# Side loads of a decode-attention backward pass, moved from SyncE's load queue to GpSimd's store queue

## The chip, the cores and the metric

The kernel runs on one core of a Trainium2 chip. A core has five engines with instruction streams of their own: TensorE (PE; its weight loads are shown as PEld), VectorE (DVE), ScalarE (ACT), GpSimd (POOL) and SyncE (SP). They wait for each other through semaphores. 16 DMA engines move data between the chip's main memory and the on-chip buffers. A transfer is issued by an instruction of SP, ACT or POOL and then lies in that engine's DMA queue; an engine issues its transfers in the order of its own instruction stream, and an instruction that waits holds up all that stand behind it. The metric is the device time of one execution in microseconds (us), the median of several runs.

## The reference

The forward pass is a conditioned block: `mod = silu(c) @ w_mod` gives six vectors; then layer norm, attention of one query row against a key and value cache (32 heads, 8192 positions, 192 numbers a head), and a small MLP. What is computed is the output and the gradients of nine of the inputs:

```python
h = _layernorm(x, axis=-1) * (1 + ca) + sa
x = x + ga * _A_ref(h, A_k_cache, A_v_cache, A_wq, A_wo)   # softmax(q k) v @ wo, q = h @ wq
h = _layernorm(x, axis=-1) * (1 + cb) + sb
x = x + gb * _B_ref(h, B_w1, B_w2, B_w3, B_w4)
...
_out, _vjp = jax.vjp(_f, A_x, A_k_cache, A_v_cache, A_wq, A_wo, B_w3, B_w4, c, w_mod)
_grads = _vjp(grad_out)
```

The two caches are 100.7 MB each, and so are their gradients dK and dV. One query row makes all products rank one, so the kernel moves much and computes little for each byte.

## The kernel before, in words

**Stage one** (to about 560 us) runs the forward pass over the heads: K and V tiles come in through SP, and nothing large goes out.

**Stage two** (the rest) runs backward over 64 half heads. The loop `for s in range(NS)` counts them in s; one s handles a tile of 128 x 32 x 192 numbers, 1.57 MB. For each s it reads one V tile, five ahead (`load_v`, L328, on SP), multiplies it by a row of the gradient on DVE (`mul_q`, L1092), sums on PE (`tree_q`, L1111), makes dP and dS on DVE (L347, L1458), writes a dK tile on DVE (`dk_part`, L1127) and a dV tile on PE and ACT (`dv_groups`, L1122 and L1123), and stores both through POOL (`dk_store`, L1412, and `dv_store`, L1408). The stores leave from five buffers used in turn (KC, VB2, QT, KE, KD; the trace names them by their tiles KB, VB and qs_bc), so a dK or dV write can wait until an earlier store from the same buffer has landed.

**Side work** is cut into steps by hand and laid into the loop. `at(s0, n, g)` puts n steps of a generator g at the times s0, s0 + 0.25, ... in units of s; `slot()` is called four times in each s and takes the steps that are due. So a plan time of 8.5 means the third slot of s = 8, which stands behind `dk_store(8)` and ahead of `dv_store(8)` in the text. One s takes some 12.5 us. The side work is:

- `g_ld(n)` loads a tile of wo (0.49 MB, `load_wo`, L203, SP), `g_do(n)` transposes it on PE (L903) for the next pair of heads, and `g_dwo(n)` overwrites it with the gradient of wo (DVE, L1255) and stores it (L1225, POOL). There are two buffers, wo_st, so a load waits until the store of the tile before the last has landed.
- `g_dq` and `g_wm` work on chunks of wq and w_mod (0.98 MB each, 13 in all). `next_w()` (L1152, SP) loads the chunk after the present one into one of two buffers, w_st and stg; the first transposes that read it come a little over two s later. The chunk is overwritten with its gradient and stored by `put` (L1225).
- Four finished stores (two tiles of dwo, two chunks of dw_mod) are held back in a list and issued near the end by `g_held` (L1229, POOL).

The order of the instructions is fixed as written for four engines, and not for POOL:

```python
ORDER = {mybir.EngineType.PE, mybir.EngineType.DVE, mybir.EngineType.Activation, mybir.EngineType.SP}
...
ctx.enter_context(tc.manual_schedule(engines=ORDER))
```

POOL's own order is chosen when the kernel is built.

Of the kernel before, what the change touches and what calls it, by code (L numbers as in the profile page):

```python
# [20 lines left out]
def kernel(  # L21
# [26 lines left out]
    nc = tc.nc  # L48
# [16 lines left out]
    NT = HQ // 2  # L65
    PW = 2 * DH
    CW = 2 * PW
# [49 lines left out]
    def tcol(n, name, dtype=FP32):  # L117
        return tmp.tile([P, n], dtype, name=name)
# [34 lines left out]
    def layernorm_bwd(dn, n, r, add, out, name):  # L153
        pr = col(2 * ND, "lb_pr")
        V_.tensor_copy(out=pr[:, 0:ND], in_=dn)
        V_.tensor_tensor(out=pr[:, ND : 2 * ND], in0=dn, in1=n, op=ALU.mult)
        s = mean_cols(pr, 2, "lb_s")
        t1 = col(ND, "lb_t1")
        V_.tensor_scalar(out=t1, in0=n, scalar1=s[:, 1:2], scalar2=s[:, 0:1], op0=ALU.mult, op1=ALU.add)
        t2 = col(ND, "lb_t2")  # L160
        V_.tensor_tensor(out=t2, in0=dn, in1=t1, op=ALU.subtract)
        V_.scalar_tensor_tensor(out=out, in0=t2, scalar=r[:, 0:1], in1=add, op0=ALU.mult, op1=ALU.add)
# [13 lines left out]
    def store_vec(src, dram, name):  # L176
        tp = psS.tile([NF, P], FP32, name="sv_t", tag="s")
        T_.transpose(out=tp[0:ND, :], in_=src, identity=ident_f)
        rows = tmp.tile([ND, P], BF16, name="sv_rows", tag="rows")
        V_.tensor_copy(out=rows, in_=tp[0:ND, :])  # L180
        nc.gpsimd.dma_start(out=dram.rearrange("o (i p) -> (o i) p", p=P), in_=rows)
# [4 lines left out]
    wo_v = A_wo.rearrange("(t p c) r -> t p c r", p=P, c=3)  # L186
# [8 lines left out]
    def load_w(view3, lo, hi):  # L195
        w = wst.tile([P, ND, CW], BF16, name="w_st", tag="w", bufs=1)
        nc.sync.dma_start(out=w[:, :, 0 : hi - lo], in_=view3[:, :, lo:hi])
        return w

    def load_wo(t):  # L200

        w = wst.tile([P, 3, D], BF16, name="wo_st", tag="wo")
        nc.sync.dma_start(out=w, in_=wo_v[t])  # L203
        return w


# [120 lines left out]
    def load_v(h, t, v):  # L327
        nc.sync.dma_start(out=v, in_=V_hd[h][:, t * JH : (t + 1) * JH, :])  # L328
        return v
# [25 lines left out]
    TL = NT - 1  # L355
# [20 lines left out]
    with tc.tile_pool(name="vs", bufs=3) as vsp, tc.tile_pool(name="ft", bufs=2) as ft, \  # L376
            tc.tile_pool(name="psM", bufs=2, space=PS) as psM, tc.tile_pool(name="psO", bufs=2, space=PS) as psO, \
            tc.tile_pool(name="psR", bufs=2, space=PS) as psR:
        def load_k(h, t):
            kb = KB[(2 * h + t) % NKB]  # L380
            if (h, t) == (H1, 1):
                for j in (0, JQ):
                    nc.sync.dma_start(out=kb[:, j : j + JQ, :], in_=K_hd[h][:, JH + j : JH + j + JQ, :])
            else:
                nc.sync.dma_start(out=kb, in_=K_hd[h][:, t * JH : (t + 1) * JH, :])
            return kb
# [131 lines left out]
        w = load_w(wq_v, 0, CW)  # L518
# [3 lines left out]
        X, os_, wo_l = {0: {"k": [load_k(0, 0), load_k(0, 1)], "v": [load_v(0, 0, VB[0])]}}, {}, {}  # L522
# [15 lines left out]
        with tc.manual_schedule(engines=ORDER):  # L538
            for i in range(H1):
# [4 lines left out]
                t = (i - 4) // 2  # L544
                late = i % 2 == 0 and t >= 0
# [402 lines left out]
            def dw4_dve(dst, a0, lo, hi):  # L948
                for a in range(lo, hi):
                    V_.tensor_scalar(out=dst[:, (a - a0) * D : (a - a0 + 1) * D], in0=dbo_bc, scalar1=g_[:, a : a + 1], scalar2=None, op0=ALU.mult)  # L950

            def dw4_store(dst, lo, n):
                nc.gpsimd.dma_start(out=dw4_v[:, lo : lo + n, :], in_=dst[:, 0 : n * D].rearrange("p (a r) -> p a r", a=n))
# [87 lines left out]
    def do_of(h):  # L1041
        return do_r[:, (TL - h // 2) % NDR, (h % 2) * DH : (h % 2 + 1) * DH]
# [101 lines left out]
    def next_w():  # L1144
        if wseq:
            view, n = wseq.pop(0)
            if cur.setdefault("n", 0) % 2 == 0:
                w = wst.tile([P, ND, CW], BF16, name="w_st", tag="w", bufs=1)
            else:
                w = bst.tile([P, ND, CW], BF16, name="stg")  # L1150
            cur["n"] += 1
            nc.sync.dma_start(out=w, in_=view[:, :, n * CW : (n + 1) * CW])  # L1152
            cur["next"] = w

    def g_bcast(src, n, out):
# [21 lines left out]
        yield  # L1177

    def g_ld(n):
        wo_l[TL - n] = load_wo(TL - n)  # L1180
        yield

    def g_chunk(b, first, v3, rows, dst, n, acc, lay):
# [43 lines left out]
    def g_held():  # L1227
        out, w = held.pop(0)
        nc.gpsimd.dma_start(out=out, in_=w)  # L1229
        yield  # L1230

    def g_dq(t):
        acc = tcol(3, "dq_acc")
        if t == TL:
            V_.tensor_copy(out=acc, in_=dq_x)
        for lo, hi, M, b in ((0, P, M1[:, 2 * t, 0:DH], 0), (0, P, M1[:, 2 * t + 1, 0:DH], 2), (0, 64, M2[0:64, t, 0:DH], 1), (64, P, M2[64:128, t, 0:DH], 1)):
            h = 2 * t + (1 if (b == 2 or lo == 64) else 0)
            if h == H1:
                continue
            junk = bst.tile([P, DH], FP32, name="dq_junk")  # L1240
            V_.tensor_tensor_reduce(out=junk[lo:hi, :], in0=M, in1=do_of(h)[lo:hi, :], scale=1.0, scalar=0.0, op0=ALU.mult, op1=ALU.add, accum_out=acc[lo:hi, b : b + 1])
        dq = tcol(3, "dq")
        V_.scalar_tensor_tensor(out=dq, in0=acc, scalar=SCALE, in1=ckS[:, 3 * t : 3 * t + 3], op0=ALU.mult, op1=ALU.subtract)
        yield from g_chunk(t % 2, t % 2 == 1, dq, ha, dwq_v, t // 2, dha, HEADS)

    def g_wm(n):
        for b in range(2):
            g = 2 * n + b
            yield from g_chunk(b, b == 0, dmod[:, 3 * g : 3 * g + 3], sc, dwm_v, n, dsc, PLAIN)
# [29 lines left out]
    def g_dw3(lo, n):  # L1279
        dw3_v = out_6.rearrange("(i p) n -> p i n", p=P)  # L1280
        o3 = bst.tile([P, ND, CW], BF16, name="stg").rearrange("p a r -> p (a r)")
        for i in range(n):
            V_.tensor_scalar(out=o3[:, i * F : (i + 1) * F], in0=du_bc, scalar1=n2[:, lo + i : lo + i + 1], scalar2=None, op0=ALU.mult)
        if lo == 0:
            dw4_dve(o3[:, n * F : n * F + D], 11, 11, 12)
            dw4_store(o3[:, n * F : n * F + D], 11, 1)
        nc.gpsimd.dma_start(out=dw3_v[:, lo : lo + n, :], in_=o3[:, 0 : n * F].rearrange("p (a r) -> p a r", a=n))
        if lo + n == ND:
            next_w()
        yield  # L1290

    def g_finish_x():
        V_.tensor_copy(out=d_sa, in_=dha)
        V_.tensor_tensor(out=d_ca, in0=dha, in1=n0, op=ALU.mult)
        d_n0 = tcol(ND, "d_n0")
        V_.scalar_tensor_tensor(out=d_n0, in0=ca, scalar=1.0, in1=dha, op0=ALU.add, op1=ALU.mult)
        dx = tcol(ND, "dx")
        layernorm_bwd(d_n0, n0, r0, dx1, dx, "lb0")
        yield
        store_vec(dx, out_1[0], "dx")  # L1300
        yield

    def g_finish_c():
        t = tcol(ND, "dc_t")
        V_.tensor_scalar(out=t, in0=sig, scalar1=-1.0, scalar2=1.0, op0=ALU.mult, op1=ALU.add)
        V_.tensor_tensor(out=t, in0=t, in1=c_c, op=ALU.mult)
        V_.scalar_tensor_tensor(out=t, in0=t, scalar=1.0, in1=sig, op0=ALU.add, op1=ALU.mult)
        V_.tensor_tensor(out=t, in0=t, in1=dsc, op=ALU.mult)
        store_vec(t, out_8, "dc")
        yield  # L1310
# [4 lines left out]
    def at(s0, n, g):  # L1315
        plan.extend((s0 + 0.25 * k, g) for k in range(n))

    CW0, CWS, DO0 = 14.0, 3.5, 16.5
    d = g_do(1)
# [5 lines left out]
    d = g_do(2)  # L1325
# [2 lines left out]
    at(6.5, 1, g_dwo(1))  # L1328
    at(6.75, 4, g_bcast(du, NF, du_bc))
    at(7.75, 1, g_dw3(0, 2))  # L1330
    at(8.0, 1, g_ld(3))
    at(8.25, 2, g_small())
    at(8.75, 1, g_dwo(2))
    at(9.0, 3, g_do(3))
    at(9.75, 1, g_dw3(2, 2))
    at(10.0, 1, g_dwo(3))
    at(10.75, 1, g_ld(4))
    at(11.25, 1, g_dw3(4, 1))
    at(13.0, 3, g_do(4))
    at(13.75, 1, g_dwo(4))  # L1340
    for n in range(5, NT):
        d = DO0 + CWS * (n - 5) if n < NT - 2 else 47.75 + 0.75 * (n - NT + 2)
        at(d - 3.25, 1, g_ld(n))
        at(d, 3, g_do(n))
        at(d + 0.75, 1, g_dwo(n))
    late = list(range(GX, NWM))
    k, t = 0, TL
    while t >= 0 or late:
        if t >= 0 and not (late and k % 3 == 2):
            wseq.append((wq_v, t // 2))  # L1350
            at(CW0 + CWS * k, 5, g_dq(t))
            at(CW0 + CWS * k + 1.25, 5, g_dq(t - 1))
            t -= 2
        else:
            wseq.append((wm_v, late[0]))
            at(CW0 + CWS * k, 10, g_wm(late.pop(0)))
        k += 1
    at(CW0 + CWS * k - 1.0, 2, g_finish_x())
    for n in range(GX):
        wseq.append((wm_v, n))  # L1360
        at(CW0 + CWS * k, 10, g_wm(n))
        k += 1
    at(CW0 + CWS * k - 1.0, 1, g_finish_c())
    for s0 in (60.25, 60.75, 61.25, 62.25):
        at(s0, 1, g_held())
    plan.sort(key=lambda p: p[0])
    NP = len(plan)
# [83 lines left out]
    for s in range(NS):  # L1451
        h, t = ht(s)
# [6 lines left out]
            out=dS4,  # L1459
# [111 lines left out]
```

## Time and profile before

| what | value |
|---|---|
| median of 3 runs | 1391.4 us (1387.59 to 1393.44) |
| the profiled execution | 1390.66 us |
| its span, first to last instruction | 1388.9 us |
| DMA moved | 569.38 MB, mean 410 GB/s |
| q1, SP's queue | 342.03 MB, 60.0% of the DMA engines' span |
| q0, POOL's queue | 224.89 MB, 38.6% |
| busy share PE / DVE / ACT / POOL | 84% / 80% / 66% / 8% |
| granted TensorE clock, mean | 0.732 |

The profile is of one execution. Times in it count from the first instruction; 1.8 us of the execution lie outside the span. The view of stretches gives, for each stretch of time, each engine's busy time (with the number of instructions in brackets), the granted TensorE clock, the busy share of the 16 DMA engines and the rate in GB/s. The view of waits gives, for an engine and a line, what it waited for, the total, the number of waits and the longest. The timeline gives start, duration, engine, line and operation; a DMA's row is its issue, not its transfer. "POOLq" and "SPq" are the queues' own instructions.

### The profile page before, as it was taken

To read this page: it belongs to the slowest core of one execution; us is meant where nothing else is said; L and a number is where in the kernel's file an instruction comes from. 1 tells how busy PE (TensorE), PEld (TensorE's weight loads), DVE (VectorE), ACT (ScalarE), POOL (GpSimd) and SP (SyncE) were. 2 spreads that over 40 slices of the span, in tenths; PEclk is the share of its full clock that TensorE was granted. 3 is DMA by queue.
4 is the path that set the end of the run, shared out by engine and by line. 5 is a ranking of instruction groups with operands and counts; after the bars stand their busy time and mean duration, and the time that the engine had idled before them with its cause. 6 is when DMAs were issued, how large, how long until landed. Compare 5 with 4: busy or idle time off the path is not lost.

```text
span 1388.9 us, 30507 instructions
## 1 busy us (share of the span) xinstructions
PE 1163.4 (84%) x12712; PEld 735.9 (53%) x12712; DVE 1109.2 (80%) x1455; ACT 911.8 (66%) x2007; POOL 108.1 (8%) x196
## 2 busy tenths in 40 slices
PE   3989989999998999988868888788579896987974
PEld 2777777778787777633323444344334343433421
DVE  4999989999999999976757676677577766876784
ACT  0777777777777778866545666566466565755754
POOL 0000000000000000111111111011011111110011
PEclk8999999999999999755555565555665555755555
DMA  9999999999999999699999999999999999999989
GB/s 381 398 422 425 418 408 411 423 421 415 424 418 422 414 417 380 231 421 426 424 424 425 427 423 427 425 422 415 425 408 424 412 421 392 417 426 423 425 359 379
DMA packets 76872, 569.38 MB, mean 410 GB/s; under 512 B 7422, under 2 KB 25198, under 8 KB 37182
## 3 DMA queue, kind: packets, MB, share of 16 engines
q1 hardware_dynamic: 51594, 342.03, 60.0%
q0 software_dynamic: 24624, 224.89, 38.6%
q8 instruction: 99, 1.62, 0.4%
q10 hardware_dynamic: 516, 0.51, 0.1%
q14 instruction: 39, 0.32, 0.1%
HBM read 340.97 MB, written 226.44 MB: 409 GB/s over the span
## 4 chain that ended last, share of the span: by engine, by line
issue 41%; DVE 25%; DMA 18%; PE 8%; POOL 5%; ACT 1%; POOLq 0%; SPq 0%; DVEq 0%; ACTq 0%
DVE prod L333 10%; DMA KB<-in_A_k_cache_dram 9%; DVE prod L337 5%; DMA out_dram<-KB 5%; DMA out_dram<-qs_bc 4%; DVE vs L403 4%; PE mp L425 2%; POOL out_dram L1412 2%; PE half_ps L343 2%; POOL out_dram L1408 2%; PE mp L430 1%; POOL out_dram L1225 1%; DVE KB L1127 1%; DVE pq L1092 1%; DMA w4b<-in_B_w_dram 1%
## 5 line engine op out<-in xcount | busy, mean ns | idle before, releaser
L1111 PE MATMUL dot_ps<-pq,ident_bf 128*128 128x256 bf16 x1494 | 369.9, 389 | 27.4 <-DVE dP L347 25.6
L410 ACT ACTIVATE vs<-VB,Ef 128x192 bf16<-128x192 bf16 x840 | 303.6, 447 | 0.0
L1123 ACT CAST KB<-dv_ps 128x768 bf16<-128x768 f32 x312 | 241.1, 806 | 82.7 <-PE dv_ps L1122 81.9
L1111 PEld LDWEIGHTS <-ident_bf 128*128 128x128 bf16 x1494 | 148.2, 122 | 176.1 <-issue 139.2
L1122 PE MATMUL dv_ps<-do_r,er_b 1*128 1x192 bf16 x2016 | 223.5, 331 | 4.3 <-ACT KB L1123 2.7
L333 DVE TENSOR_TENSOR prod<-KB,qs_bc 128x6144 bf16<-128x6144 bf16 x62 | 207.9, 3352 | 24.1 <-DMA KB<-in_A_k_cache_dram 20.4
L1127 DVE TENSOR_TENSOR KB<-qh,dS 128x3072 bf16<-128x3072 bf16 x74 | 128.1, 1753 | 97.7 <-DMA out_dram<-KB 79.9
L425 PE MATMUL mp<-vs,KB 128*128 128x193 bf16 x1984 | 188.8, 247 | 3.9 <-ACT vs L410 2.6
L425 PEld LDWEIGHTS <-KB 128*128 128x128 bf16 x1984 | 168.6, 97 | 13.0 <-DMA KB<-in_A_k_cache_dram 5.3
L904 ACT COPY wT<-wT_ps 128x1024 bf16<-128x1024 bf16 x82 | 79.1, 964 | 108.4 <-PE wT_ps L903 108.1
L1122 PEld LDWEIGHTS <-er_b 1*128 1x128 bf16 x2016 | 69.1, 104 | 142.4 <-issue 139.9
L343 PE MATMUL half_ps<-prod,ident_bf 128*128 128x256 bf16 x744 | 95.1, 279 | 43.3 <-DVE prod L337 43.2
L403 DVE TENSOR_TENSOR vs<-VB,E 128x1728 bf16<-128x1728 bf16 x120 | 123.7, 1052 | 0.3 <-ACT vs L410 0.3
L1092 DVE TENSOR_TENSOR pq<-VB,do_r 128x3072 bf16<-128x3072 bf16 x66 | 115.5, 1750 | 0.0
L337 DVE TENSOR_TENSOR prod<-prod 128x3072 bf16<-128x3072 bf16 x62 | 108.7, 1754 | 1.0
L1092 DVE TENSOR_TENSOR pq<-KB,do_r 128x3072 bf16<-128x3072 bf16 x62 | 108.4, 1749 | 0.0
L430 PE MATMUL mp<-vs,KB 128*64 128x193 bf16 x1968 | 105.7, 250 | 0.0
L343 PEld LDWEIGHTS <-ident_bf 128*128 128x128 bf16 x744 | 72.9, 100 | 61.7 <-issue 52.9
L1123 ACT CAST VB<-dv_ps 128x768 bf16<-128x768 f32 x96 | 75.1, 806 | 38.1 <-PE dv_ps L1122 37.8
L1123 ACT CAST qs_bc<-dv_ps 128x768 bf16<-128x768 f32 x104 | 80.3, 806 | 24.8 <-PE dv_ps L1122 24.3
L390 ACT ACTIVATE E<-S_h,negm 128x256 bf16<-128x256 f32 x31 | 15.8, 508 | 113.8 <-DVE negm L561 111.5
L430 PEld LDWEIGHTS <-KB 128*64 128x64 bf16 x1968 | 78.8, 109 | 19.8 <-issue 19.4
(380 smaller groups left out, 1212.3 us busy)
## 6 DMA issues: line engine op xcount, KB each, us to landing
VB<-in_A_v_cache_dram SPq DMA_DIRECT2D x93, 1536.0 KB
out_dram<-KB POOLq DMA_DIRECT2D x74, 1536.0 KB, 18.0
KB<-in_A_k_cache_dram SPq DMA_DIRECT2D x63, 1536.0 KB
KB<-in_A_v_cache_dram SPq DMA_DIRECT2D x29, 1536.0 KB
out_dram<-qs_bc POOLq DMA_DIRECT2D x25, 1536.0 KB, 16.9
out_dram<-VB POOLq DMA_DIRECT2D x25, 1536.0 KB, 18.1
wo_st<-in_A_wo_dram SPq DMA_DIRECT2D x31, 480.0 KB
w_st<-in_A_wq_dram SPq DMA_DIRECT2D x12, 960.0 KB
```

The costliest lines, as they stand in the source:

```text
L333: V_.tensor_tensor(out=prod, in0=src, in1=vec[:, None, :].to_broadcast([P, JH, DH]), op=ALU.mult)
L337: V_.tensor_tensor(out=prod[:, :, 0:HW], in0=prod[:, :, 0:HW], in1=prod[:, :, DH - HW : DH], op=ALU.add)
L343: T_.matmul(ps, lhsT=ident_bf, rhs=prod[:, :, k : k + TF], start=(k == 0), stop=(k == w - TF))
L403: V_.tensor_tensor(out=vs[:, 0:n, 0:DH].rearrange("p j (a b) -> p j a b", b=4), in0=v[:, v0 : v0 + n, :].rearrange("p j (a b) -> p j a b", ...
L410: A_.activation(out=vs[:, k, 0:DH], in_=v[:, v0 + k, :], func=ACT.Copy, scale=Ef[:, j0 + k : j0 + k + 1])
L425: T_.matmul(mp[:, 0:MW], lhsT=kb[:, j0 + k, 0:P], rhs=vs[:, k, 0:MW], start=(q == 0 and k == 0), stop=(z and k == JQ - 1), skip_group_chec ...
L430: T_.matmul(mp[p0 : p0 + 64, MO : MO + MW], lhsT=kb[:, j0 + k, P:DH], rhs=vs[:, k, 0:MW], start=False, stop=(z and k >= JQ - 2), skip_grou ...
L1092: V_.tensor_tensor(out=pq[:, q], in0=v_l[s][:, q * JQ : (q + 1) * JQ, :], in1=do_of(ht(s)[0])[:, None, :].to_broadcast([P, JQ, DH]), op=AL ...
L1111: T_.matmul(ps[:, q * JQ : (q + 1) * JQ, :], lhsT=ident_bf, rhs=pq[:, q, :, k : k + TS], start=(k == 0), stop=(k == w - TS), skip_group_ch ...
L1122: T_.matmul(ps[:, b, k * DH : (k + 1) * DH], lhsT=er[p0 : p0 + 1, 2 * m + k, :], rhs=doh[p0 : p0 + 1, :], start=True, stop=True)
L1123: A_.copy(out=dV4[:, 2 * q : 2 * q + 2, m * PW : (m + 1) * PW], in_=ps[:, :, 0:PW])
L1127: V_.tensor_tensor(out=dK[:, lo:hi, :].rearrange("p j (a b) -> p j a b", b=4), in0=qh.rearrange("p (a b) -> p a b", b=4)[:, None, :, :].to ...
```

## The change

wq and w_mod chunks (all 13) and the wo tiles from n = 3 on (13 of them) are loaded through POOL's queue, where only stores are now. The tiles n = 1 and 2 stay on SP, as do all V tiles. Some steps move in the plan:

- `g_ld(3)` from 8.0 to 8.5; `next_w` after the last dw3 store becomes a step of its own, a quarter of an s later;
- wo tile 13: its three steps from 44.5 to 44.0, tile 15 from 48.5 to 49.0, with its load 2.25 instead of 3.25 ahead of it (46.75 instead of 45.25);
- the chunks of the end from 49.0, 52.5 and 56.0 to 49.75, 53.0 and 56.25; `g_finish_x` from 51.5 to 52.25, `g_finish_c` from 58.5 to 58.75;
- the held stores from 60.25, 60.75, 61.25 and 62.25 to 58.0, 58.0, 58.75 and 60.25.

```diff
-    def load_wo(t):
+    def load_wo(t, eng=nc.sync):
         w = wst.tile([P, 3, D], BF16, name="wo_st", tag="wo")
-        nc.sync.dma_start(out=w, in_=wo_v[t])
+        eng.dma_start(out=w, in_=wo_v[t])
...
-            nc.sync.dma_start(out=w, in_=view[:, :, n * CW : (n + 1) * CW])
+            nc.gpsimd.dma_start(out=w, in_=view[:, :, n * CW : (n + 1) * CW])
...
-        wo_l[TL - n] = load_wo(TL - n)
+        wo_l[TL - n] = load_wo(TL - n, nc.gpsimd if n > 2 else nc.sync)
...
         nc.gpsimd.dma_start(out=dw3_v[:, lo : lo + n, :], in_=o3[:, 0 : n * F].rearrange("p (a r) -> p a r", a=n))
+        yield
         if lo + n == ND:
             next_w()
-        yield
+            yield
...
-    at(8.0, 1, g_ld(3))
+    at(8.5, 1, g_ld(3))
...
-    at(11.25, 1, g_dw3(4, 1))
+    at(11.25, 2, g_dw3(4, 1))
...
-        d = DO0 + CWS * (n - 5) if n < NT - 2 else 47.75 + 0.75 * (n - NT + 2)
-        at(d - 3.25, 1, g_ld(n))
+        d = DO0 + CWS * (n - 5) if n < NT - 3 else (44.0, 47.75, 49.0)[n - NT + 3]
+        at(d - (3.25 if n < NT - 1 else 2.25), 1, g_ld(n))
...
+    cw = [CW0 + CWS * i for i in range(10)] + [49.75, 53.0, 56.25]
...
-    at(CW0 + CWS * k - 1.0, 2, g_finish_x())
+    at(cw[k] - 0.75, 2, g_finish_x())
...
-    at(CW0 + CWS * k - 1.0, 1, g_finish_c())
-    for s0 in (60.25, 60.75, 61.25, 62.25):
+    at(58.75, 1, g_finish_c())
+    for s0 in (58.0, 58.0, 58.75, 60.25):
         at(s0, 1, g_held())
```

In the lines left out, `CW0 + CWS * k` becomes `cw[k]`.

More of the change, by code (lines that the diff above doesn't have):

```diff
@@ L1350 @@
             wseq.append((wq_v, t // 2))
-            at(CW0 + CWS * k, 5, g_dq(t))
-            at(CW0 + CWS * k + 1.25, 5, g_dq(t - 1))
+            at(cw[k], 5, g_dq(t))
+            at(cw[k] + 1.25, 5, g_dq(t - 1))
             t -= 2
@@ L1355 @@
             wseq.append((wm_v, late[0]))
-            at(CW0 + CWS * k, 10, g_wm(late.pop(0)))
+            at(cw[k], 10, g_wm(late.pop(0)))
         k += 1
-    at(CW0 + CWS * k - 1.0, 2, g_finish_x())
+    at(cw[k] - 0.75, 2, g_finish_x())
     for n in range(GX):
         wseq.append((wm_v, n))
-        at(CW0 + CWS * k, 10, g_wm(n))
+        at(cw[k], 10, g_wm(n))
         k += 1
-    at(CW0 + CWS * k - 1.0, 1, g_finish_c())
-    for s0 in (60.25, 60.75, 61.25, 62.25):
+    at(58.75, 1, g_finish_c())
+    for s0 in (58.0, 58.0, 58.75, 60.25):
         at(s0, 1, g_held())
```

## The prediction

> **What bounds the kernel now.** I read the page's slices first. Their DMA row shows the 16 DMA engines full nearly throughout; POOL and SP do little else than issue transfers, and PE, DVE and ACT all have idle time. So the time is the bytes at some 424 GB/s, plus whatever makes the DMA engines run dry. I then cut the last 260 us into stretches of 5 us and looked for low rates (columns: us, five engines with counts, clock, DMA share, GB/s):
>
> ```profile
> 1165.00:1170.00 5.00, 5.00 (x45) 2.35 (x44) 0.00 (x0) 2.72 (x4) 0.00 (x0) 0.50 1.01 422
> 1170.00:1175.00 5.00, 3.81 (x27) 1.33 (x25) 2.40 (x2) 3.76 (x5) 0.00 (x0) 0.50 0.87 354
> 1175.00:1180.00 5.00, 0.00 (x0) 0.00 (x0) 4.91 (x14) 0.14 (x1) 1.11 (x2) 0.50 0.94 276
> 1180.00:1185.00 5.00, 4.37 (x32) 2.28 (x32) 4.88 (x8) 2.13 (x3) 0.00 (x0) 0.57 0.93 352
> ...
> 1325.00:1330.00 5.00, 0.48 (x5) 0.21 (x5) 4.43 (x13) 0.00 (x0) 0.53 (x1) 0.50 0.61 256
> 1330.00:1335.00 5.00, 4.86 (x33) 2.01 (x30) 4.54 (x5) 3.57 (x5) 0.92 (x2) 0.50 0.78 321
> 1335.00:1340.00 5.00, 5.00 (x33) 1.53 (x30) 4.97 (x5) 3.49 (x5) 0.44 (x2) 0.50 0.76 322
> 1340.00:1345.00 5.00, 4.69 (x29) 2.04 (x30) 4.93 (x6) 3.64 (x6) 1.29 (x3) 0.50 0.86 358
> ```
>
> Two holes. Between 600 and 1170 every stretch has a DMA share of 0.98 or more: there nothing can be gained except by moving bytes faster. What opens the holes is in the waits of DVE and of SP's queue:
>
> ```profile
> DVE KB L1127 <- DMA out_dram<-KB: 79.9, 21, 10.6
> SPq L203 <- DMA out_dram<-wo_st: 38.7, 4, 22.7
> SPq L1152 <- DMA out_dram<-stg: 26.2, 5, 9.0
> ```
>
> Compute waits for stores to land, never for a V tile: no V load is a releaser in DVE's list. And SP, in order, once stands 22.7 us behind one wo load that waits for a store; the V load behind it comes late:
>
> ```profile
> 1150.67 0.33 SPq L328 DMA_DIRECT2D VB<-in_A_v_cache_dram  x1
> 1173.71 0.33 SPq L203 DMA_DIRECT2D wo_st<-in_A_wo_dram  x1
> 1174.13 1.14 SPq L328 DMA_DIRECT2D VB<-in_A_v_cache_dram  x1
> ```
>
> This is tile 15 (load at 45.25), which takes the buffer of tile 13, stored by the step at 45.25 as well (POOL issue 1157.16).
>
> **The change part by part.** The sum is made against the profiled execution, 1390.66 us, which is 0.7 below the median of 1391.4.
>
> *The hole at 1170.* Against 424 GB/s the three stretches lack 70, 148 and 72 GB/s: 290 x 5 / 424 = 3.4 us. SP no longer waits there, its V load (3.7 us of work) can start near 1165, when DVE has freed the buffer, and tile 15 is loaded 2.0 s after tile 13's store (46.75 against 44.75), some 25 us, where such stores land in 9.0 to 24.1 us. Between 0 and -3.4, I take **-3.4**.
>
> *The hole at 1325.* 168, 103, 102 and 66 GB/s are lacking: 439 x 5 / 424 = 5.2 us. DVE had waited until 1324.14 for a store, then no stores were ready. The held stores, 2 x 0.49 and 2 x 0.98 MB or 7.0 us of DMA, now come at 1341.65 to 1359.04, when DMA is full again (423 GB/s from 1345). At 58.0 the two wo stores stand right behind the dV store at 1315.08 and fill 2.3 us of the first stretch; the chunk at 58.75 stands behind 1334.59 and fills some 2 more; the fourth, at 60.25, replaces a wo store. The last ACT copy ends at 1372.3 and the DMA engines drain for 13 us more, so what they do earlier comes off the end. Between 0 and -5.2, I take **-4.3**.
>
> *The fourth wo tile (n = 3).* Before, SP issued it at 660.91 and PE waited only 0.4 us for it at 672.81. Now it stands in POOL's queue at 8.5, right behind this dK store:
>
> ```profile
> 669.39 0.56 POOL L1412 DMA_DIRECT2D out_dram<-qs_bc  x1 [9.02 <-DVE x L1274]
> 670.48 0.53 POOL L181 DMA_DIRECT2D out_dram<-sv_rows  x1 [0.53 <-DVE sv_rows L180]
> 672.62 0.55 POOL L1408 DMA_DIRECT2D out_dram<-VB  x1 [1.60 <-ACT VB L1123]
> ...
> 669.39 17.49 DMA out_dram<-qs_bc
> ```
>
> The last line is of the chain of waits: that store landed 17.49 us later, at 686.88. The tile lands with it (its own 1.2 us against 1.2 us that SP no longer takes), so PE stands at its transposes for some 14 us, and everything behind them in PE's order waits too: the rest of s = 9. That need not cost 14 us, since DMA has work meanwhile. Counted from the trace's transfers, 5.5 MB are outstanding at 673; the V load of 675.42 and the dK store of 680.42 need only DVE and come as before, 3.1 MB more. 8.7 MB last 20.4 us, to 693.4. The next store (684.97 before, 12.2 us after PE's step) would come at 699. That is a hole of 5.7 us; the end of the backlog thins out rather than stops. Ends: 0 if a backlog covers it, +14 if nothing does. I take **+5**, near the count.
>
> *Other loads.* Tile 4 (10.75, about 695.6 on POOL) is behind stores that took 18 to 22 us; it lands by 718, PE reads it at 723: no cost, 5 us of margin. All others lead by 2.25 to 3.25 s, 28 to 40 us, against 12 to 24 us for these stores from issue to landing: nothing. On POOL each issue takes 0.55 to 0.88 us; behind it stand dK and dV stores which wait 8 us on average for DVE and ACT anyway: nothing. If that cover were gone, 26 x 0.7 = 18 us of POOL's time, still not DMA's. Waits for the freed buffer move to POOL, but the stores were issued 28 us earlier: nothing.
>
> *Bytes.* A chunk row of 1536 bytes is one packet of 65.4 ns in SP's queue (8320 of them in stage two). POOL's stores of the same chunks go as packets of 4608 bytes in 184.8 ns, 61.6 per row: 8320 x 3.8 / 16 = 2.0 us less if loads are packed alike; likewise 0.8 us for wo (3840 bytes in 154.4 ns against 7680 in 294). No load of this shape lies in POOL's queue. Between 0 and -2.8, I take half, **-1.5**.
>
> A rule that speaks against moving loads to POOL: the Trainium skill, "DMA: Bandwidth & Descriptors", section "SWDGE vs HWDGE vs iDMA", says that GpSimd writes its descriptors into on-chip memory which VectorE can lock it out of. The trace shows POOL issues of 0.53 to 0.88 us with DVE 80% busy; even a delay of one long DVE instruction (3.4 us) per load would by that rule change only tile 3's wait, and the sum by under 3 us.
>
> The sum: 1390.66 - 3.4 - 4.3 + 5 - 1.5 = **1386.5 us**.
>
> **The rivals.**
>
> 1. *Tile 3's wait is hidden.* The backlog or an earlier landing covers it: 1386.5 - 5 = 1381.5. For it: DMA stayed full through every DVE wait for a store from 600 to 1165. Against: the count above, and the hole at 1175, which followed a stop of 7.7 us.
>
> 2. *The holes move and don't close.* The change only renames the queue. Both holes follow a wait of DVE for a store (until 1172.60 and 1324.14), which more work in the store queue does not shorten. Then 1390.66 + 5 - 1.5, about 1394, or 1390 without tile 3's loss. Against: in the first hole SP's queue was held by the wo load, in the second held stores were at hand. The Trainium skill, same page, section "Issuing engines are not separate DMA queues", says that the issuing engine saves issue time alone since all share the 16 DMA engines: by it the time stays at 1391. The full DMA share from 600 to 1165 agrees with it, the 22.7 us wait in SP's order doesn't.
>
> 3. *POOL becomes the blocked queue: slower.* POOL's order is not fixed as written. In stage one it was pulled far ahead:
>
> ```profile
> 478.00 0.52 POOL L611 DMA_DIRECT2D q_d<-qs_bc  x1 [20.34 <-ACT vs L401]
> 483.73 0.52 POOL L613 DMA_DIRECT2D q_rows<-q_d  x1 [5.22 <-DMA q_d<-qs_bc]
> 489.37 0.57 POOL L492 DMA_DIRECT2D eT_d<-er  x1 [5.12 <-ACT vs L401]
> ```
>
> L613 belongs two heads behind L611 and yet stands right behind it, waiting. If each load stood so behind the store that frees its buffer, POOL would wait 10 to 19 us for the landing with dK and dV stores behind it, and its queue would run empty: about 2 us until new stores move (a 640 KB store on an idle queue landed in 3.6 us, of which 1.5 is its bytes). 24 loads x 2.1 = 50 us, half of it under V loads: +25, with tile 3 in time: 1381.5 + 25 = 1406. It decides once less than one store lies between. Against: in stage two the held wo store was ready at 1207.9 and POOL often idle, and yet it was issued at 1341.65, in its written place.
>
> **How the numbers follow.** Forecast 0.38, rival 1 0.30, rival 2 0.15, rival 3 0.17. The forecast's own range is 1383 to 1391. The range of 8 in 10 takes in rival 1 with its uncertain bytes and the lower part of rival 3: 1378 to 1400. A change of under 0.5% (1384.4 to 1398.4) can't be told from none here. Faster: most of rival 1 (0.26) and a quarter of the forecast (0.10), 0.36. Slower: rival 3 and little else, 0.18. Within: 0.46.
>
> **What would show it.** Right: SP's waits on L203 and L1152 are gone but for two tiles; DMA share 0.98 or more at tile 15's place; the stretches after the last V load at 400 GB/s or more; one PE wait of some 14 us at L903 near 673, with a hole near 695. If that PE wait is absent, POOL's order differs from the text. POOL waits for out_dram<-stg or wo_st of 10 us and more, again and again, would show rival 3. The forecast is wrong if holes of other origin appear, or if the last stores, not the drain, set the end.

## The result, and the profile after

The changed kernel takes 1406.4 us in the median (1404.37 to 1414.48, 6 runs); the kernel before took 1389.8 us beside it. The ratio is 1.0125 (95% interval 1.0107 to 1.0142), so 17 us slower. Forecast were 1386.5 us and a range of 1378 to 1400: wrong in sign and in size. The profiled execution of after took 1405.57 us with a span of 1403.6, 14.7 more than before's 1388.9.

The page's rate over 40 slices and its two large queues, after:

```profile
GB/s 382 394 424 424 418 423 421 415 427 416 425 417 413 414 404 315 295 429 427 324 403 427 421 417 416 420 412 420 407 407 424 407 418 412 381 409 425 425 424 348
q1 hardware_dynamic: 41194, 322.86, 55.7%
q0 software_dynamic: 28784, 244.07, 42.1%
```

19 MB have gone from SP's queue (q1, 342.03 MB before) to POOL's (q0). Slice 20 (667 to 702 us) is down at 324 GB/s, and most slices behind it stand a few GB/s below 424. Stretches of 5 us in after, with the columns of the prediction's table:

```profile
1190.00:1195.00 5.00, 0.84 (x9) 0.26 (x8) 3.74 (x5) 1.79 (x3) 0.01 (x1) 0.50 0.56 239
1195.00:1200.00 5.00, 0.71 (x6) 0.58 (x6) 4.83 (x16) 0.00 (x0) 2.52 (x4) 0.50 0.82 295
1200.00:1205.00 5.00, 5.00 (x35) 2.32 (x34) 4.96 (x6) 2.61 (x3) 0.00 (x0) 0.50 1.00 351
1325.00:1330.00 5.00, 5.00 (x30) 1.80 (x29) 3.25 (x8) 3.02 (x5) 0.00 (x0) 0.50 1.01 411
1330.00:1335.00 5.00, 4.29 (x36) 2.52 (x35) 4.96 (x7) 3.50 (x6) 2.13 (x4) 0.50 1.00 426
1335.00:1340.00 5.00, 5.00 (x43) 2.57 (x42) 3.21 (x3) 3.19 (x6) 0.00 (x0) 0.50 1.01 426
1340.00:1345.00 5.00, 4.27 (x25) 1.36 (x23) 4.65 (x12) 3.00 (x4) 1.12 (x2) 0.50 1.01 417
```

After runs some 12 to 20 us late here, so the places in the program have to be compared, not the clock times. The hole that stood at 1325 is closed, as forecast: from 1325 to 1365 the rate is 411 to 432 GB/s. The hole that stood at 1170 is not. It followed a stop of DVE for a store's landing, and the same stop stands 18.7 us later in after. DVE's row in before, then in after:

```profile
1172.60 3.43 DVE L1127 TENSOR_TENSOR KB<-qh,dS 128x3072 bf16<-128x3072 bf16 x2 [7.69 <-DMA out_dram<-KB]
```

```profile
1191.26 3.43 DVE L1127 TENSOR_TENSOR KB<-qh,dS 128x3072 bf16<-128x3072 bf16 x2 [9.31 <-DMA out_dram<-KB]
```

Around it 185, 129 and 73 GB/s are lacking, 387 x 5 / 424 = 4.6 us, where it was 3.4 us before. The fourth wo tile behaves as the prediction said. POOL's timeline, then PE's:

```profile
669.09 0.56 POOL L1414 DMA_DIRECT2D out_dram<-qs_bc  x1 [9.05 <-DVE x L1274]
669.76 0.54 POOL L203 DMA_DIRECT2D wo_st<-in_A_wo_dram  x1
...
679.34 0.53 POOL L1414 DMA_DIRECT2D out_dram<-KB  x1 [5.92 <-DVE KB L1127]
700.46 0.53 POOL L1410 DMA_DIRECT2D out_dram<-KB  x1 [20.59 <-ACT qh L1071]
```

```profile
688.47 1.03 PE L903 MATMUL wT_ps<-ident_bf,wo_st 128*128 128x128 bf16 x8 [15.89 <-DMA wo_st<-in_A_wo_dram]
```

PE stands 15.9 us, POOL has nothing to store between 679 and 700, and the DMA engines run dry:

```profile
690.00:695.00 5.00, 5.00 (x32) 2.37 (x30) 1.80 (x2) 3.26 (x5) 0.00 (x0) 0.50 0.71 301
695.00:700.00 5.00, 5.00 (x32) 2.10 (x32) 1.22 (x3) 3.40 (x6) 0.00 (x0) 0.61 0.01 5
700.00:705.00 5.00, 4.89 (x40) 2.21 (x37) 4.96 (x7) 4.14 (x8) 1.82 (x3) 0.73 0.78 315
```

From 680 to 720 after moves 4.3 MB less than before did, 10.1 us at 424 GB/s.

Holes are only a part. Each packet's duration is in the trace, so the DMA engines' time behind 600 us can be split: **idle**; **usual**, the sum of the packets, each taken at the usual duration of its size (460 ns for 12288 bytes, 178 for 4608, 65 for 1536); and **slow**, what the packets took beyond that. All sums are divided by 16, in us of the profiled executions; a constant error of the idle part drops out of differences. "Ratio" is to the kernel before, from all runs:

| kernel | ratio, 95% interval | idle | usual | slow |
|---|---|---|---|---|
| before | 1 | 0.5 | 776.7 | 11.7 |
| after | 1.0125 (1.0107 to 1.0142) | 10.6 | 773.4 | 19.6 |
| e1, tile 3 back on SP | 1.0116 (1.0085 to 1.0147) | 5.3 | 772.5 | 21.7 |
| e2, plan alone | 0.9989 (0.9971 to 1.0008) | -1.4 | 777.6 | 12.8 |
| e3, queue alone | 1.0104 (1.0087 to 1.0121) | 3.9 | 773.2 | 22.7 |
| e4, chunks alone on POOL | 1.0022 (1.0013 to 1.0031) | 1.4 | 771.9 | 18.5 |
| e5, tiles alone on POOL | 1.0008 (0.9995 to 1.0021) | -0.1 | 774.1 | 12.9 |
| e9, before with tile 3 moved | 1.0044 (1.0026 to 1.0061) | 6.3 | 778.1 | 13.5 |
| e16, as e1, chunk loads in 3 pieces | 1.0112 (1.0093 to 1.0130) | 7.2 | 770.2 | 25.5 |

After against before: idle +10.1, usual -3.3, slow +7.9, together the span's 14.7. The rows are packed three to a packet, as hoped, and save 3.3 us; slower packets take more than twice that back. The profiled executions of e1, e3 and e5 lie 4 to 5 us under the medians of their kernels, so these three rows show too little.

### The profile page after: what moved, and what is told of

It reads as the page before. It is cut to its first block, busy times and chain, and to the rows that moved or that the text cites. A ratio compares the mean times of both kernels' runs of the same rounds, so it can differ in the third digit from the quotient of the medians.

```text
span 1403.6 us, 30447 instructions
## 1 busy us (share of the span) xinstructions
PE 1167.6 (83%) x12712; PEld 737.6 (53%) x12712; DVE 1109.8 (79%) x1455; ACT 912.0 (65%) x2007; POOL 127.4 (9%) x222
## 4 chain that ended last, share of the span: by engine, by line
issue 33%; DVE 23%; DMA 23%; PE 12%; POOL 5%; ACT 2%; SPq 0%; POOLq 0%; DVEq 0%; ACTq 0%
DVE prod L333 9%; DMA KB<-in_A_k_cache_dram 9%; DMA out_dram<-KB 6%; DVE prod L337 5%; DVE vs L403 3%; DMA out_dram<-VB 3%; DMA out_dram<-qs_bc 3%; PE mp L425 3%; PE dot_ps L1111 2%; PE half_ps L343 2%; POOL out_dram L1414 2%; PE mp L430 1%; POOL out_dram L1410 1%; DMA wo_st<-in_A_wo_dram 1%; PE dv_ps L1122 1%
## 5 line engine op out<-in xcount | busy, mean ns | idle before, releaser
L425 PEld LDWEIGHTS <-KB 128*128 128x128 bf16 x1984 | 169.1, 98 | 13.8 <-DMA KB<-in_A_k_cache_dram 5.3
```

The source lines that it names most:

```text
L425: T_.matmul(mp[:, 0:MW], lhsT=kb[:, j0 + k, 0:P], rhs=vs[:, k, 0:MW], start=(q == 0 and k == 0), stop=(z and k == JQ - 1), skip_group_chec ...
```

## The experiments

Diffs are against the kernel after unless another is named.

**e1: the fourth tile back on SP.**

```diff
-        wo_l[TL - n] = load_wo(TL - n, nc.gpsimd if n > 2 else nc.sync)
+        wo_l[TL - n] = load_wo(TL - n, nc.gpsimd if n > 3 else nc.sync)
-    at(8.5, 1, g_ld(3))
+    at(8.0, 1, g_ld(3))
```

> The kernel after, with one load back: wo tile 3 is read through SP at plan time 8.0, as before; all else as after. Theory 1 (late tile): tile 3 is 10 of the 16.7 us that the change costs, since between 680 and 720 the DMA engines of the kernel after moved 4.2 MB less than before, or 9.9 us at 424 GB/s. Then this kernel takes 1406.4 - 9.9 = 1396.5 us, PE's 15.9 us wait for wo_st near 672 is gone, and some 6.8 us above before remain. Rival: DMA has a fixed total of work and PE's stop is made good later in any case, so the time stays above 1403.

1406.4 us (1398.69 to 1414.26), ratio 1.0116. Theory 1 falls as the main cause: the loss is there without the late tile. The interval is too wide to tell a gain of 0 from one of 5 us.

**e2: the plan without the queue.** As e1, and all side loads on SP.

```diff
-            nc.gpsimd.dma_start(out=w, in_=view[:, :, n * CW : (n + 1) * CW])
+            nc.sync.dma_start(out=w, in_=view[:, :, n * CW : (n + 1) * CW])
-        wo_l[TL - n] = load_wo(TL - n, nc.gpsimd if n > 2 else nc.sync)
+        wo_l[TL - n] = load_wo(TL - n, nc.sync)
```

> The plan of after (steps moved, held stores earlier), but all side loads through SP, and wo tile 3 at 8.0. Theory 2 (the queue costs, the plan gains): the hole near 1325 closes (5.2 us) and the one near 1170 mostly (3.4 us), no load lies in the stores' queue: 1389.8 - 5.3 - 3 = 1381 to 1385 us. Rival (the plan only moves the holes): the hole of after near 1190 (3.8 us) appears here too, and with it the gain at 1325 is all that is left or less: 1386 to 1390.

1389.9 us, ratio 0.9989, the rival's time, but not by the hole that it named: stretches of 2.5 us with a DMA share below 0.93 cost 5.9 us in before (up to 1375) and 1.5 here. Both holes are closed, and the time is the same. The stop of DVE is still there, and longer, but DMA stays full through it:

```profile
1176.30 3.43 DVE L1127 TENSOR_TENSOR KB<-qh,dS 128x3072 bf16<-128x3072 bf16 x2 [10.52 <-DMA out_dram<-KB]
```

```profile
1170.00:1175.00 5.00, 4.67 (x32) 1.50 (x29) 0.00 (x0) 3.46 (x5) 0.00 (x0) 0.50 0.99 419
1175.00:1180.00 5.00, 0.00 (x0) 0.00 (x0) 3.71 (x5) 1.00 (x2) 0.00 (x0) 0.50 1.00 420
```

SP had issued a V load at 1165.8 us, a chunk load right behind it and a tile load at 1179.4; of the 4.1 MB that moved from 1176 to 1186, 1.3 were of these two side loads. The plan does no harm and brings nothing that can be measured.

**e3: the queue without the plan.** The kernel before, chunks and the tiles from n = 4 on through POOL's queue.

> The plan of before with the queue alone changed: chunks and the wo tiles from n = 4 on through POOL's queue, tile 3 on SP at 8.0 as before. Theory 2 (the queue costs): packets slower than their usual duration cost 27 us of DMA time in stage two and before in the kernel after against 20 in before by the trace, and both old holes stay or grow: 1389.8 + 7 - 3.3 for packed rows + 3 for stores that wait behind loads = 1396 to 1400 us. Rival (the queue is free, only tile 3 and the plan cost): 1389.8 - 3.3 - up to 3.4 for the hole of 1170 = 1383 to 1387.

1406.3 us, ratio 1.0104, beyond both expectations. The loss of the whole change is the queue's.

**e4: chunks alone on POOL.** As e1, all wo tiles on SP.

> The kernel after with all wo tiles back on SP (tile 3 at 8.0) and only the 13 chunks on POOL. If the cost of the queue goes with the bytes of the loads that lie in it, the chunks are 12.8 of 19.2 MB and give two thirds of what is left after tile 3: about 1381 to 1385 of the plan alone plus 2/3 of 12, so 1390 to 1393 us. If the wo tiles (one each 2.5 half heads, right ahead of a store of the other buffer) make the cost, it stands within 2 us of the plan alone.

1393.9 us, ratio 1.0022, some 4 us above the plan alone. So the tiles make 12 of the 17 us, or they only seem to; e5 tells.

**e5: tiles alone on POOL.** As e1, chunks on SP.

> The plan of after, chunks on SP, only the 12 wo tiles from n = 4 on through POOL's queue (5.9 MB). Theory 4 (SP's queue runs empty): between 610 and 1330 us SP's queue had no packet in work in 60 us of before, 61 of the plan alone, 216 with the chunks on POOL, 249 with chunks and tiles; in such time packets took 2 to 3% longer than usual and a stop of DVE opened a hole. With the tiles alone SP keeps the chunks, its empty time should stay under 120 us and the time within 3 us of the plan alone: 1388 to 1393. Rival (the tiles themselves do it: chunks cost 4 us over the plan alone, tiles 12 on top; a tile stands in POOL's queue right ahead of a dV store in each 2.5 half heads): 1398 to 1402.

1393.3 us, ratio 1.0008; the rival falls. Chunks alone cost 0.33% over the plan alone and tiles alone 0.19%; both together cost 1.27%. The loss appears when both leave SP.

**e6: loads through ACT's queue.** As e1, with `nc.scalar` where after has `nc.gpsimd` for the loads.

> The plan of after, tile 3 on SP, and chunks and tiles 4 on through ACT's queue in place of POOL's, so they stand neither ahead of stores nor with the V loads. If the loss of the move comes from loads that lie in order ahead of stores in POOL's queue, it is gone here: 1387 to 1392. If it comes from SP's queue being left with V loads alone (theory 4 in its narrow form), it stays: 1398 to 1406. ACT's issues (25 of them) and waits are a cost of their own of 0 to 3 us.

1429.5 us, ratio 1.0269, worse than either theory allowed. ACT's queue also carries er_b, 8 KB that PE needs in each s. PE's waits, ACT's queue and PE's timeline:

```profile
PE dv_ps L1122 <- DMA er_b<-eT_d: 121.4, 11, 18.6
```

```profile
707.52 0.39 ACTq L1152 DMA_DIRECT2D w_st<-in_A_wq_dram  x1
708.01 1.12 ACTq L367 DMA_DIRECT2D er_b<-eT_d  x1
719.29 0.48 ACTq L367 DMA_DIRECT2D er_b<-eT_d  x1
```

```profile
738.55 0.51 PE L1122 MATMUL dv_ps<-do_r,er_b 1*128 1x192 bf16 x8 [18.55 <-DMA er_b<-eT_d]
```

The small load stands behind a chunk of 0.98 MB in its queue (by the packets' records the chunk's run from 711 to 737 us, and er_b's follow from 736 to 738.5), and PE waits for it 11 times, 121 us in all. The run says nothing on theory 4; it shows what a large load does to a small one behind it.

**e7: the other way round.** As e2, and `put` (L1225) stores through `nc.sync`.

> The other way round: plan of after, all side loads on SP, and the stores of dwo, dwq and dw_mod that are not held (19 stores, 13.7 MB, or so) moved from POOL's queue to SP's. Theory 4: POOL's queue carries twice the bytes of SP's in stage two (216 against 113 MB); evening them out leaves SP's queue empty for less than 61 us and gives 0 to 4 us: 1386 to 1390. Rival: SP, in order, now waits for DVE's gradient before it can issue the next V load, V loads come late and holes open: 1393 to 1405.

1398.8 us, ratio 1.0060 (1.0040 to 1.0080): the rival. SP's queue is empty (under 2% of the traffic in a stretch of 1 us, 610 to 1330) for 13 us instead of 64, and yet the side loads now stand behind stores that wait for DVE (73 us of waits for wo_st and w_st at L1225 in SP's queue). PE's waits:

```profile
PE wT_ps L903 <- DMA wo_st<-in_A_wo_dram: 23.6, 3, 16.3
```

**e8: the held stores alone.** The kernel before, with

```diff
-    for s0 in (60.25, 60.75, 61.25, 62.25):
+    for s0 in (58.0, 58.0, 58.75, 60.25):
```

> The kernel before with nothing changed but the times of the four held stores (58.0, 58.0, 58.75, 60.25 in place of 60.25, 60.75, 61.25, 62.25). The prediction's step gave 4.3 us for filling the hole of 1325 to 1345: 1386.5. Theory 5 (the end is DVE's, not DMA's): from 1325 to 1372 DVE is busy 44.4 of 47 us in before and 44.2 with the plan alone, and the last stores are issued at 1371.1 and 1371.6; the hole lies beside DVE's work and its filling is worth only what the drain behind 1372 gets shorter, at most 3 us, less what the stores delay DVE's last wait: 1389 to 1392, no difference.

1390.3 us, ratio 0.9993 (0.9980 to 1.0007): theory 5. Before and then e8, the stretch behind 1325 (third number pair: DVE), and the last store's issue:

```profile
1325.00:1372.00 47.00, 38.30 (x243) 13.70 (x243) 44.41 (x46) 32.18 (x44) 9.79 (x17) 0.50 0.90 372
```

```profile
1371.08 0.53 POOL L1412 DMA_DIRECT2D out_dram<-VB  x1 [1.14 <-DVE VB L1127]
```

```profile
1325.00:1372.00 47.00, 38.99 (x246) 13.86 (x244) 43.35 (x44) 33.25 (x45) 8.70 (x15) 0.50 0.98 408
```

```profile
1370.68 0.53 POOL L1412 DMA_DIRECT2D out_dram<-VB  x1 [1.14 <-DVE VB L1127]
```

The DMA share rises from 0.90 to 0.98, the hole is filled, and the last store comes at the same time: DVE works 44.4 of 47 us in before, so the issue of the last store is set by DVE, not by DMA. The end behind it comes hardly sooner. Between 1380 and 1385 the DMA share falls from 1.00 to 0.48, and yet the last packet ends at 1385.9 us instead of 1386.8; why the rest takes so long, no run here shows.

**e9: the fourth tile alone.** The kernel before, tile 3 through POOL's queue at 8.5.

> The kernel before with one load changed: wo tile 3 through POOL's queue at 8.5 in place of SP's at 8.0. In the trace of after this load makes PE wait 15.9 us and the DMA engines miss 4.2 MB, 9.9 us at 424 GB/s; yet the kernel after with tile 3 back on SP has the same median as after, 1406.4. Theory 1 (lost DMA time is lost): 1391 + 9.9 = 1401. Rival (given back: DMA work that falls behind is caught up where the engines would else be slow or dry, as at 1170 and 1325): 1391 to 1394.

1398.2 us, ratio 1.0044, or 6.1 us (3.6 to 8.5). PE waits 14.7 us for the tile, and the DMA engines miss 9.7 us between 680 and 720. Two thirds of it reach the end; neither theory had the size. In the kernel after, whose loss is larger anyway, the same wait can't be told from nothing (e1).

**e10 to e13: with one kind of load left out.** e10 and e11 keep the handle of the tile before the last in place of a load; e12 and e13 do the same with the two chunk buffers, which the first two chunks still fill, through SP:

```diff
-        wo_l[TL - n] = load_wo(TL - n, nc.gpsimd if n > 2 else nc.sync)
+        w = wo_keep[n - 2] if n > 3 else load_wo(TL - n)
+        wo_keep[n] = w
+        wo_l[TL - n] = w
```

> Leaves out the loads of wo tiles 4 to 15 (5.9 MB; the gradient of the tile before the last is transposed in their place, so dO and what follows from it is of other numbers); chunks through POOL's queue, plan of after. SP's queue has V loads alone, as with chunks and tiles both on POOL, but no tile lies in POOL's queue. To be read against the next run, which has the chunks on SP. Theory 4 (what costs is an SP queue that has V loads alone): this one is 10 to 14 us slower than the next, as chunks and tiles together are (1.16% against -0.1%). Rival (the tiles in POOL's queue cost on their own beside the chunks): 3 to 5 us slower, as the chunks alone are.

> Leaves out the same 12 tile loads; chunks on SP. 5.9 MB less are 13.9 us at 424 GB/s: 1390 - 13.9 = 1376 if all of it lay on the path that sets the end, up to 1382 if DVE's tail behind 1325 covers a part of it. The theories differ in the run before this one.

> Leaves out 11 of the 13 chunk loads (10.8 MB, 25.5 us at 424 GB/s; the first two come through SP, the later steps work on what lies in the two buffers); tiles 4 to 15 through POOL's queue, plan of after. Here too SP's queue has V loads alone. With no side loads in POOL's queue but 5.9 MB of tiles, packets should be slow beside loads in POOL's queue for 20 to 30 us of time and 1.5 to 2.5 us in all, as with the tiles alone (2.2 us). 1392 - 25.5 = 1366.5 if only bytes count (rival); theory 4: SP's queue empty for over 200 us between 610 and 1330 and 1371 to 1378.

> Leaves out the same 11 chunk loads as the run with tiles on POOL; tiles on SP. The control of that run, which took 1365.8 us. If tiles in POOL's queue cost nothing while chunks are not there: 1364 to 1368. If they cost by their bytes what chunks cost without tiles (9 us for 12.8 MB, so 4 us for 5.9 MB): 1361 to 1363.

Without tiles: 1383.9 us (ratio 0.9950, 0.9931 to 0.9968) with the chunks on POOL, 1374.9 (0.9883, 0.9864 to 0.9901) with them on SP. The chunks cost 0.67%, 9 us, where they cost 0.33% with the tiles on SP. Without chunks: 1365.8 (0.9820, 0.9803 to 0.9837) with the tiles on POOL, 1362.1 (0.9803, 0.9785 to 0.9821) with them on SP: 0.17%, at the edge of what can be told. With V loads alone in SP's queue, 5.9 MB on POOL so cost 0.2%, 12.8 MB 0.7%, and 18.7 MB (e1 over e2) 1.3%. Theory 4 in its strict form (an SP queue of V loads alone costs 10 to 14 us, whatever lies on POOL) falls with e12; what is left of it is that the same load costs more there once SP has nothing but V loads.

**e14: V tiles on POOL.** As e2, and 11 of the V loads through POOL's queue.

```diff
-            v_l[s + 5] = load_v(*ht(s + 5), v_buf(s + 5))
+            v_l[s + 5] = load_v(*ht(s + 5), v_buf(s + 5), nc.gpsimd if s >= 5 and s % 5 == 0 else nc.sync)
```

> The plan of after with all side loads on SP, and in their place 11 of the V tiles (s + 5 = 10, 15, ... 60; 17.3 MB) through POOL's queue. Theory 6 (reads in the stores' queue split the traffic into time of reads alone and time of writes alone): between 610 and 1330 us at least nine tenths of the traffic is reads in 23 us of before and 58 to 60 us of the kernels with chunks and tiles on POOL, writes alone in 110 and 250 us, and reads alone run 8% slow in all of them; with V tiles on POOL these times grow too, packets are 5 us or more slower in all than with the plan alone (12.8), and the time is 1398 to 1406. Rival (the chunks' own form, rows of 1536 bytes that POOL packs three to a packet, is what slows): V tiles keep their packets of 12288 bytes on either queue, so 1389 to 1393.

1391.5 us, ratio 1.0014 (0.9999 to 1.0029). Theory 6 falls as put: 17.3 MB of reads in the stores' queue cost 0.25% over the plan alone while SP keeps its side loads, though the time with over nine tenths reads grows from 21 us to 66. The rival's time came out, 1389 to 1393. By the packets' records it is right in part: V tiles' packets through POOL took 2.3% longer than usual here and the chunks' 10.6% in after, but more of what after loses lies in the K and V stores (below).

**e15 and e16: chunk loads in pieces.** As e1; three pieces of a chunk, spread over three slots (e15), or at once (e16).

```diff
+            for a, b in ((0, 2), (2, 4), (4, 5)):
+                pend.append((w[:, a:b, :], view[:, a:b, n * CW : (n + 1) * CW]))
+            piece()
...
         prog[0] += 1
+        piece()
```

> Chunks and tiles from n = 4 on through POOL's queue as in the kernel after with tile 3 on SP (1.16% slower than before), but each chunk load is cut into three pieces of 2, 2 and 1 of its 5 rows a partition, issued in three slots one behind the other, some 3 us apart, with stores between. Theory 7 (bursts): a chunk through SP is in flight for 11.1 us, takes 21% of the bytes and leaves 79% to the stores, at 422 GB/s in all; through POOL it is in flight for 3.4 us, takes 74%, no store moves, and the rate is 396. Pieces between stores halve the bursts and give back a third to a half of the loss: 0.5 to 0.8% above before, 1398 to 1402. Rival (SP's queue, with V loads alone, has nothing to fill stops with, in whatever order POOL's queue stands): no difference, 1.0 to 1.3%. If the last piece lands after its first reader, PE's waits for w_st or stg show it.

> The control of the run before: the same three pieces, issued at once. One issue more than the whole load costs POOL 2 x 0.55 us, which lies beside its waits for DVE: 1.0 to 1.3% above before by either theory, as with the whole load.

1407.4 us (ratio 1.0120, 1.0103 to 1.0138) and 1405.4 (1.0112). No difference, and no PE wait for a chunk: theory 7, that bursts of reads are the cause, falls, and the figures that it started from were wrong as well (below). Both profiled executions lie near their medians and show what e1's did not: packets are 25 to 26 us slow in all, 14 more than before. With +6.7 us idle and -6.5 usual (a part of that is work that fell before 600 us) this is the 14.0 us by which e16's span is longer.

## Why the prediction was wrong, point by point

**"Other loads ... nothing".** This is the step that failed. Each load was asked one question: does it land before its reader? It does: but for the fourth tile, PE's waits for wo_st, w_st and stg stay under 4 us in all. The question not asked was what the load does to the traffic around it. Stage two was called bound by bytes at 424 GB/s; but with almost the same bytes to move, that rate was not kept.

Whose a packet is, its size tells: a chunk's are mostly of 4608 bytes on POOL and all of 1536 on SP, a wo tile's of 7680 or 3840, those of K and V tiles of 12288. Within one size they go in the order of issue, and by that the last packet of each chunk load in after ends 0.3 to 0.8 us ahead of the load's landing. The figures in the expectations of e14 and e15 come out when a queue's bytes are counted in the order of the packets' starts instead. By that count a chunk would be through 1.6 to 10.0 us ahead of its landing: the 16 DMA engines do not all stand at the same place of a queue. So the 58 to 60 us of reads and the 250 us of writes in the one, and the 3.4 us, the 74%, "no store moves" and the 11.1 us and 21% for SP in the other, do not hold. In stretches of 0.5 us between 610 and 1330 us, by the packets' sizes:

```
                       before         e2 plan        e1             after          e16
reads over 9/10     22 us  7.5%    21 us  7.6%    19 us 11.4%    26 us  8.8%    31 us 11.3%   slow
writes over 19/20  116 us  0.6%   128 us  0.7%   198 us  2.2%   212 us  2.1%   214 us  2.5%   slow
```

Through SP the packets of a chunk lie within 24 us in before and 21 us in e2 (from first to last, median of 13). They take 10 to 11% of the bytes in that time and the stores 68%, at 424 GB/s in all: a filler in the background. Through POOL, in after, they lie within 11 us and take 22%; the stores go on with 49% and V loads with 28%, and the rate is 407, since packets in this time are 4.6% slow in place of 0.5 to 0.6% (medians). All 13 chunk loads together are in flight for 144 us, in which 6.1 us of after's slow time lie. By kind of packet, slow time behind 600 us grows from 3.4 us to 8.7 in the K and V stores and from 0.2 to 3.3 in the chunk loads, which is as much as the packing saves. One of the worst places in after, 1098 to 1106 us (columns: packets, MB, share of the DMA engines' time):

```profile
DMA packets 394, 2.94 MB, mean 368 GB/s; under 512 B 44, under 2 KB 51, under 8 KB 217
q0 software_dynamic: 355, 2.67, 90.9%
q1 hardware_dynamic: 30, 0.25, 7.3%
```

The DMA engines are busy throughout, at 368 GB/s. Of the 2.67 MB in POOL's queue 0.76 are the chunk's and 1.92 stores; the chunk's packets take 39% longer than usual and the stores' 5%.

The Trainium skill, "DMA: Bandwidth & Descriptors", section "Queues, rings and completion order", says that each DMA engine takes turns between the queues that have work, a whole packet at a time. The shares agree: at 1536 against 12288 bytes a turn, an estimate by that rule gives a chunk on SP a ninth while stores are there; it got 10 to 11%.

At other times SP's queue is empty in after, for 265 us instead of 62. SP itself now waits almost only for DVE to free a V buffer (SP's queue, before, then after):

```profile
SPq L328 <- DVE pq L1092: 623.9, 57, 18.5
```

```profile
SPq L328 <- DVE pq L1092: 738.1, 58, 28.0
```

So when DVE stops for a store to land, as at 1190, SP has nothing in hand, and the hole opens. With the same plan and the side loads on SP, e2 has the same stop and no hole; with the chunks and tiles on POOL, e1 has the hole (371 and 271 GB/s between 1180 and 1190).

**The hole at 1170 (-3.4).** It closes in e2, and in after it stays and grows to 4.6 us. The prediction saw what held SP's queue up, but not that the side loads, once SP is free, are what fills such a stop. And e2 is not faster by more than 0.3%: its idle time is only 1.9 us less in all, and 1.1 us of slow packets and 0.9 us of usual work stand against that.

**The hole at 1325 (-4.3).** It closes, and is worth 0 (e8). I had read that ACT's last copy ends at 1372 and that DMA drains behind it, and took DMA's backlog as the end. But DVE's 44.4 us of work in 47 was in the same trace: the last store's issue can't move, whatever DMA does beside it, and behind it the drain kept its 17 to 18 us.

**The fourth tile (+5).** Right in mechanism and place: one PE wait at L903, 15.9 us (forecast 14), and a hole behind 690. Alone it costs 6.1 us (e9). That this is near +5 is in part luck: DMA missed 10.1 us there against the 5.7 counted, and in e9 a third of such a loss was made good later.

**Bytes (-1.5).** POOL packs loads as it packs stores; usual durations fall by 3.3 us, a little over the upper end. The term was undersized, and the chunk loads' slow packets take 3.1 us of it back.

**The rivals.** Rival 3 gave 1406, but not by what happened: POOL's loads stand in their written order, and its waits at L1152 and L203 come to 2.9 us in all in after. It is a hit by accident. Rival 2 has it right for the plan (0.9989). By the rule of the Trainium skill that stands beside it there ("Issuing engines are not separate DMA queues"), the issuing engine saves issue time alone; e3 shows a loss of 1.0% from the issuing engine, so by that rule alone the time of this move can't be told.

**What stays open.** Shown is that the loss is the queue's and not the plan's, that the late tile is not the main cause, that waits for the chunks and the pieces that their loads are cut into are none, and that chunks and tiles together cost more than the sum of each. In after 7.9 of 18.0 us gross, in e16 13.8 of 20.5, are packets that take longer, the K and V stores among them; the rest are holes. Why stores that run beside no read take 2.1 to 2.5% longer than usual in these kernels and 0.6% in before, and why chunk packets are slow in POOL's queue, no run here shows. More time of writes alone is not enough: e13, with most chunk loads left out, has 231 us of it, at 0.9%. Nor does any run show why the two parts cost more together.

## What to carry to other kernels

Where DMA is full, ask of a moved load not only when it lands, but what share of the bytes it takes while it is in flight, whether its packets and those beside it keep their usual duration, and what its old queue has in hand at the next stop. Compare holes by their place in the program, not by the clock, and tell packets apart by size before you say whose they are. Before a hole in DMA is priced, look for an engine that is busy through it: here DMA time beside an engine at 94% was worth nothing. Try each part of a change alone and both together: here 0.2% and 0.3% made 1.3%.

## What the runs showed of the hardware that was not expected

Time in which over nine tenths of the traffic is reads ran 7.5% slow in before, 7.6% in the plan alone and 8.8% in after (22, 21 and 26 us of it); over all kernels, e6 apart, it was 3 to 19% on 7 to 66 us. With five to seven tenths reads it was 1.1 to 2.8%. POOL packed rows of 1536 bytes three to a packet, usually of 178 ns, where SP sent each as a packet of 65 ns; but loads so packed took 10.6% longer than usual in after, and SP's 0.6% in before. The DMA engines did not work through POOL's queue in step: the packets of one chunk load in after lay within 4.2 to 15.1 us, where 0.98 MB last 2.3 us at 424 GB/s. And an 8 KB load behind a 0.98 MB load in ACT's queue came up to 18.6 us late.
